# Attention and two expert layers on one core: the build-time estimate that orders the work gets new rules, and the order changes

## The chip, the cores and the metric

The kernel runs on one core of a Trainium2 chip, as one launch. The metric is device time in microseconds (us) of that core. Engines are named as the profile names them: PE (TensorE matmul), PEld (its weight loads), DVE (VectorE), ACT (ScalarE), POOL (GpSimd), SP (SyncE, which issues most transfers).

## The reference

Linear attention with random features, then two mixture-of-experts layers, each of which takes the output of the one before. There are 4 batches, 8 heads, 576 tokens, head size 64, 128 features; the expert layers see 4 x 576 tokens of width 512 and have 8 experts with a hidden width of 1024.

```
def phi(x):                                   # x: (b, h, s, 64)
    h = x @ omega.T - sum(x * x, -1) / 2      # 128 features
    return exp(h - max(h, -1)) / sqrt(128)
kv  = einsum('bhsm,bhsd->bhmd', phi(k), v);   z = phi(k).sum(2)
num = einsum('bhsm,bhmd->bhsd', phi(q), kv);  den = phi(q) . z + 1e-6
x   = num / den
# expert layer 1
e   = argmax(x @ w_gate, 1)
out[mask_e] = prob_e * sigmoid(x @ w_output_gate)[e] * (relu(x[mask_e] @ w1[e]) @ w2[e])
# expert layer 2: the same with its own weights and without the sigmoid
```

## The kernel before

**Tiling.** Attention works on 16 pairs of heads (4 batches of 4 pairs). For a pair it projects the keys (`k_proj`, matmuls `ph<-om,kr`, then a maximum and ten exponentials into `kp`), contracts them with the values (`kv`, `pkv<-vt,kp`), projects the queries (`q_proj`), takes a maximum over partitions on POOL (`qhl<-qhh`), subtracts it on DVE, takes the exponential on ACT (`q_exp`), and contracts with `kv` (`num`, into `pa`); `den_a` to `norm` divide. The table `FORMS` gives each pair one of three forms: F keeps queries and `kv` as whole f32 (`pa<-qhh,kvr`, a matmul that the trace shows as two records); S splits both into a high and a low f32r part (`qh`, `ql`, `kvh`, `kvl`) and takes three products; R keeps it whole with another layout.

**Expert units.** For each layer and batch one unit computes the most frequent expert of the batch densely over its 576 tokens: an up contraction (`pm<-xh,wh`, `pm<-xl,wh`, `pm<-xh,wl`: 512 to 1024, 8 blocks of output, then `hh` on ACT and `hl` on DVE), and a down contraction (`pm<-hh,wh` and its two companions: 8 blocks of `hh` into each of 4 outputs). The 8 units follow each other; the three products in f32r take the place of f32 ones. Weights arrive as `wr`, ACT casts `wh`, DVE subtracts `wl`. The tokens of other experts are gathered in small groups (the `Block` of a layer: `put`, `sel`, the transposes `pst`, down to `pby`) and computed apart.

**What sets the order.** The program is written out once, at build, and each engine runs its list in that order. Between the matmuls of a unit there are slots, and into each slot `Attention.go` (L680) puts the attention step whose key is lowest among those that are admissible. The key is an entry of `WEIGHTS` or `RAW_WEIGHTS`, `PACE[9]` per pair, and a number of `TWEAKS` for that one step. Admissible is a step whose inputs the class `Estimate` (L101) has ready by then; it keeps a clock for each engine, a cost for each instruction, and a time at which each tile is free again. All instructions pass through `Engine.__getattr__` (L197), which is why almost every row of the trace has the line L208. Side streams (the routers `gate`, L729; the Block) advance when the estimate has what they yielded ready. Until the first unit begins, `fill` (L1316) writes an idle matmul on zeros (`idle<-zeros`) wherever nothing is admissible.

**PSUM.** The pool `psa`, tag `pa`, has 7 banks in the start-up and 4 afterwards (L1216, L1363). All of `pa`, `ph`, `pkv`, `pn`, `pg`, `pt`, `pc`, `ptc` and `pst` live there; a key projection takes four of them, two for its first three chunks of 128 tokens and two for the rest, each by half of the features' pair. The expert units have `pm` of their own. In the estimate a new tile takes the place of the one handed out `bufs` tiles before:

```
        if len(names) >= bufs:
            self.before[t.tensor.name] = names[-bufs]
```

**DVE and POOL.** Here the estimate starts a DVE instruction on SBUF no earlier than 1.2 after the start of the latest maximum on POOL (`hold`, L170 and L180).

Of the kernel before, what the change touches and what calls it, by code (L numbers as in the profile page):

```python
# [31 lines left out]
TW = 72  # L32
# [18 lines left out]
ORDER = 3  # L51


FORMS = "FRRRFFFSSSSSSSSS"
CW = 132
XW = 4

WEIGHTS = (-99.0, -99.0, 262.75, -267.46, 198.55, 332.25, -310.29, -471.44, -33.14, 239.82, -489.57, 351.55, -254.05, 173.97)
RAW_WEIGHTS = (-99.0, -99.0, -374.05, -379.93, 519.94, 42.51, 947.74, -153.49, 153.44, 733.35, -182.45, -952.4, -419.2, -198.78)

PACE = (0.097, 0.001, 1.054, 1.126, 886.024, 3.696, 0.265, 0.264, 1.069, 256.941, 0)

COPIES = (1, 1, 2, 1, 0, 0, 2)

START_PACE = (0.142, 0.015, 7.433)
START_COPIES = (1, 2, 0, 1, 0, 0, 0)
TWEAKS = {  # L70
    ("den_a", 1): 44.7, ("den_a", 2): 595.6, ("den_a", 3): -18.8, ("den_a", 4): 323.2, ("den_a", 5): 525.4,
    ("den_a", 6): 291.8, ("den_a", 7): -101.8, ("den_a", 8): -71.9, ("den_a", 9): 56.6, ("den_b", 0): 325.6,
    ("den_b", 1): 1.1, ("den_b", 4): 37.9, ("den_b", 5): -9.0, ("den_b", 6): 171.8, ("den_b", 7): 121.2,
    ("den_b", 8): -64.0, ("den_b", 9): -127.0, ("den_c", 0): 75.6, ("den_c", 1): -98.6, ("den_c", 2): 478.0,
    ("den_c", 4): 37.6, ("den_c", 5): -237.6, ("den_c", 6): -550.8, ("den_c", 9): 0.0, ("den_w", 0): 345.4,
    ("den_w", 1): 143.8, ("den_w", 2): 574.5, ("den_w", 3): -16.2, ("den_w", 4): -57.6, ("den_w", 5): -71.8,
    ("den_w", 6): 77.2, ("den_w", 7): 20.5, ("den_w", 8): 24.7, ("den_w", 9): 7.5, ("k_proj", 0): 107.5,
    ("k_proj", 1): -20.1, ("k_proj", 2): 135.6, ("k_proj", 3): -98.0, ("k_proj", 4): -29.4,
    ("k_proj", 5): -51.0, ("k_proj", 6): -49.7, ("k_proj", 8): 473.1, ("k_proj", 9): -623.2, ("kv", 0): -176.7,
    ("kv", 1): -125.4, ("kv", 3): 483.1, ("kv", 4): -62.8, ("kv", 7): -51.7, ("kv", 8): -203.5,  # L80
    ("kv", 9): 650.0, ("norm", 0): 643.8, ("norm", 1): 542.2, ("norm", 2): 77.4, ("norm", 3): -45.2,
    ("norm", 4): -186.2, ("norm", 5): -106.9, ("norm", 6): 227.5, ("norm", 7): 48.0, ("norm", 8): -0.4,
    ("norm", 9): -5.1, ("num", 0): 0.5, ("num", 1): -19.9, ("num", 10): 26.1, ("num", 14): 416.8,
    ("num", 16): 22.8, ("num", 17): 45.6, ("num", 18): 55.1, ("num", 2): -74.7, ("num", 3): 19.4,
    ("num", 4): -844.8, ("num", 6): 170.0, ("num", 7): -558.5, ("q_cut", 1): -198.8, ("q_cut", 11): -85.3,
    ("q_cut", 12): 60.3, ("q_cut", 13): -72.2, ("q_cut", 14): -1186.5, ("q_cut", 16): -207.1,
    ("q_cut", 17): 478.9, ("q_cut", 19): -174.8, ("q_cut", 2): 25.9, ("q_cut", 3): -306.2, ("q_cut", 4): -287.7,
    ("q_cut", 5): -24.0, ("q_cut", 6): -93.1, ("q_cut", 7): -533.3, ("q_cut", 9): -21.1, ("q_exp", 0): -237.5,
    ("q_exp", 1): 916.5, ("q_exp", 10): -245.4, ("q_exp", 11): -365.4, ("q_exp", 13): -179.8,
    ("q_exp", 14): 179.6, ("q_exp", 15): -1328.8, ("q_exp", 17): 117.8, ("q_exp", 18): 181.2,  # L90
    ("q_exp", 19): -23.4, ("q_exp", 2): 343.6, ("q_exp", 3): -348.5, ("q_exp", 5): -38.0, ("q_exp", 6): -20.7,
    ("q_exp", 7): 4.5, ("q_exp", 9): 820.0, ("q_proj", 0): -488.4, ("q_proj", 1): 984.4, ("q_proj", 10): -817.3,
    ("q_proj", 11): -497.2, ("q_proj", 12): 68.1, ("q_proj", 13): -219.8, ("q_proj", 14): -554.4,
    ("q_proj", 16): -308.5, ("q_proj", 19): 96.0, ("q_proj", 3): -28.6, ("q_proj", 4): -32.0,
    ("q_proj", 5): 11.6, ("q_proj", 6): -43.9, ("q_split", 11): -396.2, ("q_split", 14): -317.9,
    ("q_split", 15): 29.6, ("q_split", 17): -159.4, ("q_split", 18): 101.6, ("q_split", 19): -14.0,
    ("q_split", 5): 27.3, ("q_split", 6): -34.7, ("q_split", 7): -89.0, ("q_split", 9): -848.8,
}


class Estimate:  # L101
# [3 lines left out]
    def __init__(self):  # L105
        self.now = dict.fromkeys(("tensor", "vector", "scalar", "gpsimd", "sync", "dma"), 0.7)
        self.written, self.used, self.slots, self.before = {}, {}, {}, {}
        self.sums = set()

        self.window, self.work, self.slow = 0, 0.0, True  # L110

        self.hold = 0.0

        self.rows = 128

# [2 lines left out]

    def tile(self, ring, bufs, t):

        names = self.slots.setdefault(ring, [])
        if len(names) >= bufs:
            self.before[t.tensor.name] = names[-bufs]
        names.append(t.tensor.name)

    def clock(self, begin):
        while begin >= (self.window + 1) * 3.413:
# [8 lines left out]
    def run(self, engine, op, out, ins):  # L136
# [2 lines left out]
        begin = max(self.now[engine], self.ready(ins), free)  # L139
        psum = any(t.tensor.name in self.sums for t in (out, *ins))  # L140
        if op == "dma_start":
            self.now[engine] = begin + (0.45 if out.shape[0] % 128 == 0 or out.shape[0] < 64 else 0.65)
            end = self.now["dma"] = max(begin + 1.1, self.now["dma"]) + math.prod(out.shape) * 4 / 330e3
            end += 1.0
        elif engine == "tensor":
            if op == "transpose":
# [66 lines left out]
class Pool:  # L213
# [34 lines left out]
def attention_moe_moe_kernel(ctx, tc, qT, qT2, kT, vp, omst, wg1, wg2, w1a, w2a, w1b, w2b, tabs, eye, outT):  # L248
# [354 lines left out]
    class Attention:  # L603
# [15 lines left out]
        def needs(self, kind):  # L619
# [109 lines left out]
    def gate(l, b, x, again=False):  # L729
# [760 lines left out]
```

## Time and profile before

| what | value |
|---|---|
| median of 3 runs | 588.97 us (588.17 to 589.77) |
| profiled execution | 588.86 us |
| its span, first to last instruction | 587.10 us |
| mean granted clock of PE | 0.994 |
| busy: PE, PEld | 567.9 (97%), 540.7 (92%) |
| busy: DVE, ACT, POOL | 371.1 (63%), 225.3 (38%), 68.4 (12%) |
| matmul records of PE | 4519 |
| maxima on POOL | 32, 67.2 us in all |

The page comes first for who is busy; the waits of PE say what ended its idle time; the timeline of PE around such a wait says what stands before and behind it; windows give the granted clock of a stretch.

### The profile page before, as it was taken

Reading aid. Unit: us, or ns where it says so; the run is one execution under the profiler, and the core shown is the slowest. Engines: PE = TensorE matmul, PEld = TensorE weight load, DVE = VectorE, ACT = ScalarE, POOL = GpSimd, SP = SyncE. Lnnn points to the kernel's source line nnn. Section 1 sums busy time; section 2 is a strip of 40 time slices with the busy share of each in tenths; the row PEclk is TensorE's granted clock in tenths of the full one; section 3 lists DMA queues with packets and bytes.
Section 4 is the critical chain, followed back from the end, with each engine's and each line's share of the span. In section 5 each row is a group of like instructions: output and inputs, shape, how many; then the busy total and the mean of one; then the engine's idle time right before and its main releaser. Section 6 shows DMA issues by size and latency. Waiting matters only on the chain.

```text
span 587.1 us, 11426 instructions
## 1 busy us (share of the span) xinstructions
PE 567.9 (97%) x4519; PEld 540.7 (92%) x4519; DVE 371.1 (63%) x695; ACT 225.3 (38%) x503; POOL 68.4 (12%) x48
## 2 busy tenths in 40 slices
PE   8999989999999999999999999999999999999995
PEld 7887779988999999899999999999999999879995
DVE  4487678887775787487866876764545485313522
ACT  6776645224536224424353344322331232324300
POOL 3670500202001130011201210000000000000000
PEclk9999999989999999999999999999999999999998
DMA  9314376525473263283534634544243238664411
GB/s 315 105 62 129 93 231 194 155 87 171 127 171 123 80 217 89 66 272 130 177 94 124 199 103 114 137 150 136 81 118 133 93 95 250 235 218 154 122 41 45
DMA packets 96955, 82.76 MB, mean 141 GB/s; under 512 B 24576, under 2 KB 78464, under 8 KB 96896
## 3 DMA queue, kind: packets, MB, share of 16 engines
q1 hardware_dynamic: 95776, 81.78, 45.1%
q8 instruction: 37, 0.61, 0.4%
q10 hardware_dynamic: 1120, 0.19, 0.2%
q14 instruction: 22, 0.18, 0.1%
HBM read 66.36 MB, written 15.54 MB: 140 GB/s over the span
## 4 chain that ended last, share of the span: by engine, by line
PE 80%; DVE 8%; DMA 5%; issue 3%; ACT 2%; POOL 0%; SPq 0%; ACTq 0%; DVEq 0%; POOLq 0%
PE pm L208 62%; PE pkv L208 5%; PE ph L208 4%; PE pa L208 4%; DMA wr<-w1a 2%; DVE qhh L208 1%; PE pg L208 1%; DMA wr<-w2a 1%; DVE wl L208 1%; DMA qr<-qT 1%; DVE nm L208 1%; ACT wh L208 1%; PE pby L208 1%; DMA rdd<-dt 1%; ACT kp L208 1%
## 5 line engine op out<-in xcount | busy, mean ns | idle before, releaser
L208 PE MATMUL pm<-xh,wh 128*128 128x288 f32 x512 | 113.4, 303 | 1.6 <-DVE hl L208 1.3
L208 PE MATMUL pm<-hh,wh 128*128 128x288 f32 x512 | 114.2, 302 | 0.6 <-DVE y L208 0.6
L208 PE MATMUL pm<-hh,wl 128*128 128x288 f32 x512 | 111.4, 297 | 0.0
L208 PE MATMUL pm<-hl,wh 128*128 128x288 f32 x512 | 111.3, 297 | 0.0
L208 PE MATMUL pm<-xh,wl 128*128 128x288 f32 x512 | 109.6, 296 | 0.5 <-DVE wl L208 0.5
L208 PE MATMUL pm<-xl,wh 128*128 128x288 f32 x512 | 109.5, 295 | 0.0
L208 POOL PARTITION_ALL_REDUCE qhl<-qhh x32 | 67.2, 2139 | 282.8 <-DVE qhh L208 185.2
L208 ACT CAST wh<-wr 128x1024 fp32r<-128x1024 f32 (+1 forms) x72 | 67.8, 951 | 55.5 <-PE pm L208 40.5
L208 PEld LDWEIGHTS pm<-xh,wh 128*128 128x128 f32 x512 | 82.1, 189 | 5.7 <-DVE hl L208 2.3
L208 PEld LDWEIGHTS pm<-hh,wh 128*128 128x128 f32 x512 | 82.9, 190 | 4.4 <-issue 3.0
L208 DVE TENSOR_TENSOR wl<-wr,wh 128x1024 fp32r<-128x1024 f32 (+1 forms) x72 | 78.5, 1103 | 12.6 <-ACT wh L208 12.2
L208 PEld LDWEIGHTS pm<-hh,wl 128*128 128x128 f32 x512 | 83.3, 190 | 0.0
L208 PEld LDWEIGHTS pm<-hl,wh 128*128 128x128 f32 x512 | 83.2, 190 | 0.0
L208 DVE SCALAR_TENSOR_TENSOR hl<-pm,hh 128x576 fp32r<-128x576 f32 x64 | 48.4, 757 | 54.8 <-ACT hh L208 53.9
L208 PEld LDWEIGHTS pm<-xh,wl 128*128 128x128 f32 x512 | 82.4, 188 | 0.7 <-DVE wl L208 0.7
L208 PEld LDWEIGHTS pm<-xl,wh 128*128 128x128 f32 x512 | 82.3, 188 | 0.0
L208 ACT ACTIVATE hh<-pm 128x576 fp32r<-128x576 f32 x64 | 41.7, 651 | 73.3 <-PE pm L208 73.2
L208 DVE TENSOR_TENSOR y<-pm,cb 128x576 f32<-128x576 f32 (+1 forms) x33 | 24.3, 737 | 58.4 <-PE pm L208 58.3
L208 ACT ACTIVATE kp<-ph,nm 128x128 f32<-128x128 f32 x140 | 38.0, 387 | 21.1 <-DVE nm L208 19.2
L208 ACT ACTIVATE qhh<-qhh 128x576 f32<-128x576 f32 x32 | 22.1, 706 | 58.3 <-DVE qhh L208 56.1
L208 DVE TENSOR_REDUCE nm<-ph 128x3 f32<-128x384 f32 (+1 forms) x64 | 27.2, 484 | 14.2 <-PE ph L208 14.1
L208 PEld LDWEIGHTS pkv<-vt,kp 128*128 128x128 f32 x280 | 32.6, 192 | 1.5 <-ACT ev L208 0.8
(145 smaller groups left out, 580.0 us busy)
## 6 DMA issues: line engine op xcount, KB each, us to landing
wr<-w2a SPq DMA_DIRECT2D x16, 512.0 KB, 4.1
wr<-w2b SPq DMA_DIRECT2D x16, 512.0 KB, 3.9
qr<-qT SPq DMA_DIRECT2D x24, 288.0 KB, 4.3
wr<-w1a SPq DMA_DIRECT2D x12, 512.0 KB, 4.7
wr<-w1b SPq DMA_DIRECT2D x12, 512.0 KB, 3.9
vt<-vp SPq DMA_DIRECT2D x16, 325.0 KB, 4.5
kr<-kT SPq DMA_DIRECT2D x16, 288.0 KB, 4.4
xd<-xraw SPq DMA_DIRECT2D x16, 288.0 KB, 3.5
```

Of the source, the lines that this page charges most:

```text
L208: return f(*args, **kw)
```

## The change

The estimate changes in three rules. A new PSUM tile takes, of the banks whose last use is an engine's read, the one read first, instead of a fixed round; a step that needs several banks is admissible only if so many are free (`spare`, `banks`). DVE is held after each of the last eight maxima, not only the last. A transfer's cost goes by the length of its rows. The two exponentials of a router get tiles of their own, `ge` and `te`, where they were slices of `g` and `t`; the router's stream yields those. `FORMS` makes pairs 8 and 10 (batch 2, first and third pair) F instead of S. `WEIGHTS`, `RAW_WEIGHTS`, `PACE`, `COPIES` (which engine copies what), `START_PACE`, `START_COPIES` and `TWEAKS` have other numbers, so that another order results. No transfer and no maximum is added or dropped.

```
-FORMS = "FRRRFFFSSSSSSSSS"
+FORMS = "FRRRFFFSFSFSSSSS"
-COPIES = (1, 1, 2, 1, 0, 0, 2)
+COPIES = (1, 1, 1, 1, 0, 0, 2)
-START_COPIES = (1, 2, 0, 1, 0, 0, 0)
+START_COPIES = (2, 0, 0, 1, 0, 0, 0)
-    ("den_a", 1): 44.7, ("den_a", 2): 595.6, ("den_a", 3): -18.8, ("den_a", 4): 323.2, ("den_a", 5): 525.4,
+    ("den_a", 0): -615.3, ("den_a", 1): -48.5, ("den_a", 2): 148.9, ("den_a", 3): 49.8, ("den_a", 4): -124.6,
...
         names = self.slots.setdefault(ring, [])
         if len(names) >= bufs:
-            self.before[t.tensor.name] = names[-bufs]
+            old = names[0]
+            if self.banks.get(ring):
+                read = [n for n in names if n in self.seen and not self.seen[n][1]]
+                old = min(read, key=lambda n: self.seen[n][0], default=old)
+            names.remove(old)
+            self.before[t.tensor.name] = old
         names.append(t.tensor.name)
+
+    def spare(self, pool, tag):
+
+        ring = id(pool), tag
+        return pool.bufs - sum(n not in self.seen or self.seen[n][1] for n in self.slots.get(ring, ()))
...
-                    self.hold = begin + 1.2
+                    self.holds = [*self.holds[-7:], begin]
...
-                if self.hold - 1.2 < begin < self.hold and not psum:
-                    begin = self.hold
+                for h in self.holds:
+                    if h < begin < h + 1.2 and not psum:
+                        begin = h + 1.2
...
+        self.uses += 1
         for t in (out, *ins):
             name = t.tensor.name
+            self.seen[name] = self.uses, engine == "tensor"
...
+        def banks(self, kind, p):
+            if kind == "k_proj" or kind == "q_proj" and p.tiled:
+                return 4
+            return {"q_proj": 2, "num": 2, "kv": 1, "norm": 2 * p.raw, "q_exp": 2 * p.flip}.get(kind, 0)
...
                 if any(now[e] > now["tensor"] + limit for e in engines):
+                    continue
+                if est.spare(pl.psa, "pa") < self.banks(kind, self.pairs[k]):
                     continue
...
-        nc.scalar.activation(g[:, 2], g[:, 1], AF.Exp)
+        nc.scalar.activation(ge, g[:, 1], AF.Exp)
...
-            nc.scalar.activation(t[:, 5], t[:, 4], AF.Exp, scale=-1.0)
-        yield [g, t]
-        nc.vector.tensor_reduce(out=t[:, 2], in_=g[:, 2], axis=AX.X, op=ALU.add)
+            nc.scalar.activation(te, t[:, 4], AF.Exp, scale=-1.0)
+        yield [ge, te] if l == 0 else [ge]
+        nc.vector.tensor_reduce(out=t[:, 2], in_=ge, axis=AX.X, op=ALU.add)
```

The order on PE around the ninth key projection (pair 8), in the first unit; `pt` is the router's transpose of its logits `lg`, `pm` the unit. Before:

```order
L208 MATMUL pm<-hh,wh 128x288 x2
L208 MATMUL pm<-hl,wh 128x288 x2
L208 MATMUL pm<-hh,wl 128x288 x2
L208 MATMUL pt<-ident,lg 72x128 x2
L208 MATMUL ph<-om,kr 128x128 x10
L208 MATMUL pm<-hh,wh 128x288 x2
```

Now:

```order
L229 MATMUL pa<-qh,kvh 128x288
L229 MATMUL pa<-qh,kvl 128x288
L229 MATMUL pa<-ql,kvh 128x288
L229 MATMUL pm<-xh,wh 128x288 x2
L229 MATMUL pm<-xl,wh 128x288 x2
L229 MATMUL pm<-xh,wl 128x288 x2
L229 MATMUL ph<-om,kr 128x128 x10
L229 MATMUL pm<-xh,wh 128x288 x2
```

The projection has moved from the unit's down contraction into its up contraction, and no router tile stands directly ahead of it. The tenth, which stood behind a `ptc` and a `pkv`, and the thirteenth, which stood behind a `ptc`, now stand behind `pm`; the eleventh stands behind a `pkv` in both.

The order on PE around the first transposes `pst` of the second layer's Block, with tile numbers so that the blocks of `hh` can be counted; the seventh unit's down contraction is under way, and a new pair of `hh`, `hl` begins each block. Before:

```order
L208 MATMUL pm_5994<-hh_5690,wh_5734 128x288 x2
L208 MATMUL pm_5994<-hl_5691,wh_5734 128x288 x2
L208 MATMUL pm_5994<-hh_5690,wl_5735 128x288 x2
L208 MATMUL pm_5994<-hh_5723,wh_5734 128x288 x2
L208 MATMUL pm_5994<-hl_5724,wh_5734 128x288 x2
L208 MATMUL pm_5994<-hh_5723,wl_5735 128x288 x2
L208 MATMUL pst_6032<-ident_89,sel_5944 96x128 x4
L208 MATMUL pm_5994<-hh_5767,wh_5734 128x288 x2
```

Now:

```order
L229 MATMUL pm_5962<-hh_5788,wh_5702 128x288 x2
L229 MATMUL pm_5962<-hl_5789,wh_5702 128x288 x2
L229 MATMUL pm_5962<-hh_5788,wl_5703 128x288 x2
L229 MATMUL pm_5962<-hh_5838,wh_5702 128x288 x2
L229 MATMUL pm_5962<-hl_5839,wh_5702 128x288 x2
L229 MATMUL pm_5962<-hh_5838,wl_5703 128x288 x2
L229 MATMUL pst_6018<-ident_89,sel_5912 96x128 x4
L229 MATMUL pm_5962<-hh_5897,wh_5702 128x288 x2
```

Before, `pst` stood behind the fourth of the output's eight blocks of `hh`; now it stands behind the seventh, so 18 `pm` matmuls later. Between the last `ptc` ahead of it and `pst` there were 162 `pm` matmuls, and there are 180.

The order on DVE at the start of the first unit's up contraction; `xh` and `xl` are the unit's last input parts, `hl` the low part of a hidden block, `dt` a pair's denominators. Before:

```order
L208 TENSOR_TENSOR xl<-xraw,xh 128x576
L208 TENSOR_SCALAR dt<-dt 32x36
L208 RECIPROCAL dt<-dt 32x36
L208 TENSOR_TENSOR qhh<-qhh,qhl 128x576
L208 CAST qh<-qhh 128x576
L208 SCALAR_TENSOR_TENSOR hl<-pm,hh 128x576
L208 TENSOR_TENSOR wl<-wr,wh 128x1024 x2
L208 SCALAR_TENSOR_TENSOR hl<-pm,hh 128x576
```

Now:

```order
L229 TENSOR_TENSOR xl<-xraw,xh 128x576
L229 SCALAR_TENSOR_TENSOR hl<-pm,hh 128x576
L229 TENSOR_SCALAR dt<-dt 32x36
L229 RECIPROCAL dt<-dt 32x36
L229 TENSOR_TENSOR qhh<-qhh,qhl 128x576
L229 CAST qh<-qhh 128x576
L229 TENSOR_TENSOR wl<-wr,wh 128x1024
L229 SCALAR_TENSOR_TENSOR hl<-pm,hh 128x576
```

The first `hl` has moved ahead of a pair's four small and middle instructions; the second still stands behind them, with one `wl` fewer between.

## Rows read from the trace of the kernel before

**Rows 1.** The page's part 1, busy time of each engine.

```profile
PE 567.9 (97%) x4519; PEld 540.7 (92%) x4519; DVE 371.1 (63%) x695; ACT 225.3 (38%) x503; POOL 68.4 (12%) x48
```

**Rows 2.** Windows around 126 us: stretch, length, busy us (instructions), clock, DMA share, GB/s.

```profile
122.80:126.30 3.50, 2.16 (x25) 1.65 (x22) 2.19 (x5) 1.63 (x6) 0.00 (x0) 1.00 0.51 159
126.30:129.70 3.40, 3.40 (x16) 3.40 (x15) 3.26 (x8) 1.31 (x6) 0.00 (x0) 0.50 0.12 18
```

**Rows 3.** Waits of PE: waited for, total us, times, longest.

```profile
PE ph L208 <- ACT kp L208: 4.0, 4, 1.3
PE pm L208 <- DVE hl L208: 1.3, 1, 1.3
PE pst L208 <- issue: 1.2, 1, 1.2
...
PE pn L208 <- ACT qhh L208: 0.5, 1, 0.5
PE pt L208 <- ACT lg L208: 0.4, 1, 0.4
```

**Rows 4.** Timeline of PE, key projections: start, us, instruction, count, idle before.

```profile
123.10 1.16 PE L208 MATMUL ph<-om,kr 64*128 64x128 f32 x14
125.60 0.71 PE L208 MATMUL ph<-om,kr 64*128 64x128 f32 x6 [1.34 <-ACT kp L208]
126.24 0.84 PE L208 MATMUL pm<-hh,wh 128*128 128x288 f32 x2
...
141.19 1.48 PE L208 MATMUL ph<-om,kr 64*128 64x128 f32 x14
143.75 0.71 PE L208 MATMUL ph<-om,kr 64*128 64x128 f32 x6 [1.09 <-ACT kp L208]
144.39 0.53 PE L208 MATMUL pm<-hh,wh 128*128 128x288 f32 x2
...
183.87 1.39 PE L208 MATMUL ph<-om,kr 64*128 64x128 f32 x20
185.18 0.53 PE L208 MATMUL pm<-hh,wh 128*128 128x288 f32 x2
...
233.69 1.16 PE L208 MATMUL ph<-om,kr 64*128 64x128 f32 x14
236.19 0.71 PE L208 MATMUL ph<-om,kr 64*128 64x128 f32 x6 [1.35 <-ACT kp L208]
236.83 0.53 PE L208 MATMUL pm<-xh,wh 128*128 128x288 f32 x2
```

**Rows 5.** Timeline of PE at the state's transposes.

```profile
495.04 0.42 PE L208 MATMUL pm<-hh,wl 128*128 128x288 f32 x2
496.70 0.61 PE L208 MATMUL pst<-ident,sel 128*96 128x128 f32 x4 [1.24 <-issue]
```

**Rows 6.** Timeline of DVE at the same place.

```profile
495.79 0.81 DVE L208 SCALAR_TENSOR_TENSOR sel<-pos,state,sel 128x576 f32<-128x576 f32 x1
```

**Rows 7.** Chain that ended last: start, us, what.

```profile
505.68 1.58 PE pm L208 x12
...
527.53 0.97 PE pby L208 x4
```

**Rows 8.** Timeline of ACT in the start-up.

```profile
18.71 3.92 ACT L208 COPY qhh<-ph 128x288 f32<-128x288 f32 x12 [0.28 <-PE ph L208]
22.40 0.80 ACT L208 ACTIVATE qhh<-qhh 128x576 f32<-128x576 f32 x1
```

**Rows 9.** Timeline of DVE in the first unit.

```profile
82.72 0.76 DVE L208 SCALAR_TENSOR_TENSOR hl<-pm,hh 128x576 fp32r<-128x576 f32 x1
```

**Rows 10.** Tiles qhh and qhl: ns min/median/max, first and last start, form.

```profile
L208 POOL PARTITION_ALL_REDUCE qhl<-qhh x32: 1964/2042/2762, 9.9 to 349.3; - x32
L208 DVE TENSOR_TENSOR qhh<-qhh,qhl x32: 682/751/1706, 11.9 to 353.5; 128x576 f32<-128x576 f32 x32
```

More of the change, by code (lines that the diff above doesn't have):

```diff
@@ L51 @@
 ORDER = 3
-FORMS = "FRRRFFFSSSSSSSSS"
+FORMS = "FRRRFFFSFSFSSSSS"
 CW = 132
 XW = 4
-WEIGHTS = (-99.0, -99.0, 262.75, -267.46, 198.55, 332.25, -310.29, -471.44, -33.14, 239.82, -489.57, 351.55, -254.05, 173.97)
-RAW_WEIGHTS = (-99.0, -99.0, -374.05, -379.93, 519.94, 42.51, 947.74, -153.49, 153.44, 733.35, -182.45, -952.4, -419.2, -198.78)
-PACE = (0.097, 0.001, 1.054, 1.126, 886.024, 3.696, 0.265, 0.264, 1.069, 256.941, 0)
-COPIES = (1, 1, 2, 1, 0, 0, 2)
-START_PACE = (0.142, 0.015, 7.433)
-START_COPIES = (1, 2, 0, 1, 0, 0, 0)
@@ L70 @@
-TWEAKS = {
-    ("den_a", 1): 44.7, ("den_a", 2): 595.6, ("den_a", 3): -18.8, ("den_a", 4): 323.2, ("den_a", 5): 525.4,
[L72 to L97, printed above, removed]
@@ new lines @@
+WEIGHTS = (-99.0, -99.0, 465.22, -215.23, 475.57, 303.97, 62.0, -391.59, -72.09, 241.12, -272.33, 415.93, -220.17, 177.53)
+RAW_WEIGHTS = (-99.0, -99.0, -320.83, -643.41, 757.51, 23.54, 902.27, -181.77, -108.58, 760.71, -209.95, -1003.88, -544.16, -272.35)
+PACE = (0.06, 0.02, 1.043, 1.722, 1746.379, 0.527, 0.544, 0.14, 0.662, 226.645, 0)
+COPIES = (1, 1, 1, 1, 0, 0, 2)
+START_PACE = (0.008, 0.005, 9.732)
+START_COPIES = (2, 0, 0, 1, 0, 0, 0)
+TWEAKS = {
+    ("den_a", 0): -615.3, ("den_a", 1): -48.5, ("den_a", 2): 148.9, ("den_a", 3): 49.8, ("den_a", 4): -124.6,
+    ("den_a", 5): -241.3, ("den_a", 6): 9.0, ("den_a", 7): 58.2, ("den_a", 8): 39.3, ("den_a", 9): 66.5,
+    ("den_b", 0): -22.1, ("den_b", 1): -120.3, ("den_b", 2): -43.5, ("den_b", 3): -30.1, ("den_b", 4): -12.3,
+    ("den_b", 5): -27.2, ("den_b", 6): -186.1, ("den_b", 7): 8.6, ("den_b", 8): -28.8, ("den_b", 9): -156.6,
+    ("den_c", 0): 297.9, ("den_c", 1): 87.7, ("den_c", 2): 7.2, ("den_c", 3): -101.4, ("den_c", 6): 559.4,
+    ("den_c", 7): 122.8, ("den_c", 8): 892.4, ("den_c", 9): -130.8, ("den_w", 0): 65.5, ("den_w", 1): 69.5,
+    ("den_w", 4): -8.8, ("den_w", 7): 55.1, ("den_w", 8): 51.1, ("den_w", 9): 315.7, ("k_proj", 0): 43.7,
+    ("k_proj", 1): 770.1, ("k_proj", 2): 6.2, ("k_proj", 5): -102.0, ("k_proj", 6): -135.9,
+    ("k_proj", 7): -485.8, ("k_proj", 8): 201.5, ("k_proj", 9): -509.3, ("kv", 0): 800.9, ("kv", 2): -971.1,
+    ("kv", 3): 539.0, ("kv", 4): -158.3, ("kv", 5): 14.6, ("kv", 7): -1420.6, ("kv", 8): 133.2, ("kv", 9): 57.6,
+    ("norm", 0): -36.8, ("norm", 1): -2.7, ("norm", 2): -245.3, ("norm", 3): 192.2, ("norm", 5): -251.9,
+    ("norm", 6): -22.2, ("norm", 7): 56.3, ("norm", 9): -21.9, ("num", 0): 259.5, ("num", 1): 239.5,
+    ("num", 12): -74.1, ("num", 13): -3.1, ("num", 14): -402.8, ("num", 15): -45.9, ("num", 17): -1553.0,
+    ("num", 18): 464.6, ("num", 19): -484.1, ("num", 2): 16.8, ("num", 3): -58.4, ("num", 4): -48.5,
+    ("num", 7): -37.5, ("q_cut", 0): 470.8, ("q_cut", 1): 52.5, ("q_cut", 10): 287.1, ("q_cut", 11): 390.2,
+    ("q_cut", 12): -26.4, ("q_cut", 13): 125.3, ("q_cut", 14): 3.7, ("q_cut", 15): 40.2, ("q_cut", 17): 412.5,
+    ("q_cut", 18): 48.1, ("q_cut", 19): -173.6, ("q_cut", 2): -56.2, ("q_cut", 8): -8.2, ("q_exp", 1): 916.5,
+    ("q_exp", 10): 20.8, ("q_exp", 12): -67.8, ("q_exp", 13): -91.1, ("q_exp", 14): 17.5, ("q_exp", 15): -87.5,
+    ("q_exp", 16): -39.0, ("q_exp", 18): 45.7, ("q_exp", 19): 55.4, ("q_exp", 2): 1058.6, ("q_exp", 3): -69.7,
+    ("q_exp", 4): -458.6, ("q_exp", 5): 1030.3, ("q_exp", 7): 82.1, ("q_exp", 8): 1.3, ("q_exp", 9): 291.1,
+    ("q_proj", 1): -49.4, ("q_proj", 10): -249.0, ("q_proj", 11): 20.8, ("q_proj", 12): -127.1,
+    ("q_proj", 13): -109.9, ("q_proj", 14): -554.4, ("q_proj", 15): -192.8, ("q_proj", 16): -104.3,
+    ("q_proj", 2): 1419.6, ("q_proj", 3): -180.4, ("q_proj", 4): 61.9, ("q_proj", 5): -23.2, ("q_proj", 6): 6.8,
+    ("q_proj", 7): 100.9, ("q_proj", 8): -41.2, ("q_proj", 9): -222.4, ("q_split", 0): 27.2,
+    ("q_split", 1): -26.3, ("q_split", 10): -206.2, ("q_split", 11): -4.4, ("q_split", 13): 51.2,
+    ("q_split", 14): -317.9, ("q_split", 15): -589.0, ("q_split", 17): -159.4, ("q_split", 19): 38.5,
+    ("q_split", 2): 20.6, ("q_split", 3): 34.3, ("q_split", 5): -39.3, ("q_split", 6): 615.3,
+    ("q_split", 7): -40.6, ("q_split", 8): -7.0, ("q_split", 9): 848.8,
@@ L108, in __init__ @@
         self.sums = set()
+        self.banks, self.seen, self.uses = {}, {}, 0
         self.window, self.work, self.slow = 0, 0.0, True
-        self.hold = 0.0
+        self.holds = []
         self.rows = 128
@@ L141, in run @@
         if op == "dma_start":
-            self.now[engine] = begin + (0.45 if out.shape[0] % 128 == 0 or out.shape[0] < 64 else 0.65)
-            end = self.now["dma"] = max(begin + 1.1, self.now["dma"]) + math.prod(out.shape) * 4 / 330e3
+            self.now[engine] = begin + (0.42 if out.shape[0] % 128 == 0 else 0.55)
+            row = out.shape[-1] * 4
+            cost = math.prod(out.shape[:-1]) / 16e3 * (2 + row / 25 if row >= 512 else 40 if row > 256 else 10)
+            if len(out.shape) > 2 and row >= 512 or out.shape[0] == 64:
+                cost *= 1.5
+            end = self.now["dma"] = max(begin + 1.1, self.now["dma"]) + max(0.17, cost)
             end += 1.0
@@ L219, in tile @@
         t = self.pool.tile(shape, dtype, tag=tag, name=name, **kw)
+        self.estimate.banks[id(self), tag] = self.space is not None
         self.estimate.tile((id(self), tag), bufs or self.bufs, t)
@@ L754, in gate @@
         ls = pl.mp.tile([TW, NT, GW], F32, tag="ls", name="ls", bufs=1)
+        ge = pl.mp.tile([TW, NT, E], F32, tag="ge", name="ge", bufs=1)
+        te = pl.mp.tile([TW, NT, 1], F32, tag="te", name="te", bufs=1)
         first = rev[:TW]
@@ L812, in gate @@
             nc.vector.scalar_tensor_tensor(
-                out=t[:, 3], in0=t[:, 5], scalar=1.0, in1=t[:, 3], op0=ALU.add, op1=ALU.mult
+                out=t[:, 3], in0=te, scalar=1.0, in1=t[:, 3], op0=ALU.add, op1=ALU.mult
             )
```

## The prediction

> **What bounds the kernel now.** I read the page's busy times first. PE is busy 567.9 us of a span of 587.10 [rows 1], so 19.2 us at most can be won without taking work off PE; DVE, at 63%, and the others bound nothing on average. So I listed what ended PE's waits [rows 3]. The largest entry is the key projection `ph`, which waits for the exponentials `kp` four times, 4.0 us in all. The other single waits of a size that matters are one for `hl` in the first unit (1.3) and one before `pst` (1.2); what else the view lists are waits of half a microsecond, such as `pn` (0.5) and `pt` (0.4).
>
> Next, the timeline of PE at those projections [rows 4]. A projection is 20 records. One that meets no wait starts at 183.87 and the next `pm` at 185.18: 1.31 us. The ninth stops after 14 records, waits 1.34 us for `kp`, and the next `pm` starts at 126.24, that is 3.14 us after 123.10. A projection fills four banks, two of three chunks each and two of two chunks; its seven first matmuls need three of them, the eighth the fourth. That is where the records break, 14 and 6: the fourth bank was still held by what stood directly ahead (a router's `pt`, not yet read), so the eighth matmul had to take the projection's own first bank, once its exponentials were done. The same picture stands at 141.19 (3.20) and 233.69 (3.14), where a `pkv` and a `ptc` stood ahead.
>
> Last, the granted clock. Between the start-up and the end it dips once, and the windows place that: 3.50 us at 1.00 with PE busy 2.16, then 3.40 us at 0.50, that is 1.2 GHz instead of 2.4, with PE busy throughout [rows 2]. The first of these stretches holds the ninth projection's stall.
>
> **The change part by part.** The sum is made against the profiled execution, 588.86 us (the span 587.10 and 1.76 around it); the median of the runs is 0.11 above, and I carry the sum over to the median.
>
> *Key projections.* By the new order the ninth, tenth and thirteenth no longer stand behind a router's tile or a `pkv`; a `pm` block lies ahead, during which older banks are read out. What they cost over a free one is 3.14 - 1.31 = 1.83, 3.20 - 1.31 = 1.89, and 1.83 again [rows 4]: 5.55 us, all on PE's path, since PE has nothing else in its list there. The eleventh stands behind a `pkv` before and after, so I count no change for it. What is late next at the ninth is the next `hh` cast or DVE's `hl`, neither of which the timeline shows waiting when the projection runs through. Value -5.55, bounds -5.55 and -4.5 (a short wait of 0.35 left at each of three).
>
> *The half clock.* 3.40 us at half the clock do the work of 1.70 [rows 2]. If the stall ahead of it goes, so does this: -1.7, bounds -1.7 and 0. By the rows, three stalls of 1.09 to 1.35 us at key projections brought one such stretch, so the coincidence is one in three here. Beside that stands a rule of the Trainium skill, "TensorE: Matmul & The Clock Gate", Part 1: The HAM clock gate: throttled is the default and activity releases it, and the monitor's window runs freely, so where a stall falls decides as much as how long it is. The trace agrees as far as one in three goes; the rule speaks against the full 1.7, since a new stall elsewhere may fall badly, and by it the gain would be 1.7 smaller. That result is the first rival below.
>
> *The `pst` wait.* Before, `pm` x2 starts at 495.04 and at 0.132 a matmul (12 in 1.58 [rows 7]) would end at 495.30; `pst` starts at 496.70, 1.40 later [rows 5], because `sel` on DVE ends at 495.79 + 0.81 = 496.60 [rows 6]. Now `pst` stands 18 `pm` later, 18 x 0.132 = 2.37 us, and the order ahead of `sel` on DVE and of its transfer is as before. So 2.37 - 1.40 = 0.97 us to spare, and the wait goes: -1.40. Nothing in the Block behind `pst` had less slack than that: the next groups of it are not in the waits [rows 3]. Bounds -1.4 and -0.8, if `sel` comes 0.6 later still beyond the slack.
>
> *Two pairs in form F.* Pairs 8 and 10 lose 24 f32r products, 24 x 0.132 = 3.17 us, and gain 8 f32 ones of two records. A record of f32 with the same 288 columns takes 0.97 / 4 = 0.24 (`pby` [rows 7]): 16 x 0.2425 = 3.88. So +0.7 on PE; the nearest lower value, if a record of `pa` overlaps its neighbour, gives 0. DVE loses four casts, four subtractions and two of `kvl`, but it bounds nothing there: no gain counted. I take +0.7, bounds 0 and +0.7.
>
> *Start-up.* The count of idle matmuls falls from 54 to 42, but these fill waits and cost nothing by themselves. On ACT, the exponential `qhh` at 22.40 stood behind 12 copies of `ph` [rows 8]; now only 8 of these come before it, 4 x 3.92 / 12 = 1.31 us less of copies, while an exponential moves ahead of them, 0.80. So -0.5 (bounds -1.3, if that exponential finds ACT idle, and +0.5, if the filler that went leaves PE to wait where it did not). The rest of the start-up ends on the chain of routers and first weights, in which nothing changed. What hides the change of order there is that chain; if it is earlier by 1.3, that is the lower bound.
>
> *First unit.* The first `hl` ends its wait earlier: it started at 82.72 behind `dt`, `qhh` and `qh` [rows 9] and made PE wait 1.3 [rows 3]. It now stands ahead of them. The second `hl` stands behind them instead, with one `wl` less between. DVE has the same list of work up to there but for that `wl`, so the wait may only be handed on by a block. 0, bounds -1.3 and +1.3.
>
> *The router's tiles, the estimate's other rules.* `ge` and `te` change when the estimate holds the exponentials for ready; on the chip the same two instructions write the same amount. 0. The new costs of transfers and the holds work through the order only, which is priced above.
>
> *New small waits.* The small waits of before belong to its order; a new order has its own. Rows of that size are 0.4 and 0.5 [rows 3]. I add three of 0.45, +1.3, bounds 0 and +2.5, and give no credit for the old ones.
>
> Sum: -5.55 - 1.7 - 1.4 + 0.7 - 0.5 + 0 + 1.3 = -7.15. So 588.97 - 7.15 = 581.8 us. With all lower ends (-5.55 - 1.7 - 1.4 + 0 - 1.3 - 1.3 + 0 = -11.25) it would be 577.7; with a middle run of upper ends (-4.5, -0.8, +0.7, +0.5, 0, +2.5 and the clock at -1.7: -3.3) 585.7. Both ends together are unlikely; the forecast's own range is 579 to 585.7.
>
> **The rivals.**
>
> *The half clock moves instead of vanishing.* For it: a single stall of some 1.3 us in one of three places was enough. The fewer idle matmuls in the start-up leave PE to wait on exponentials, where such a stretch may begin. Against it: 54 fillers before included ones that changed nothing in the clock. Time: 581.8 + 1.7 = 583.5. Chance 0.2.
>
> *The order does not free the banks.* The bank rule is one of the estimate; on the chip the pool and the readers decide. If the eighth matmul still waits at three projections, the 5.55 and the 1.7 stay: -1.4 + 0.7 - 0.5 + 1.3 = +0.1, so 589.1. For it: the change at L116 touches no instruction. Against it: the order itself has moved those three. Chance 0.08.
>
> *DVE falls behind in the first unit (slower).* Mechanism: the first unit now carries key projections nine to eleven, the ninth in its up contraction, so DVE has their maxima, subtractions and casts to do while each block of the up contraction needs an `hl` from it. A subtraction `qhh` that meets a maximum on POOL has taken up to 1.706 us against a median of 0.751, 0.96 more [rows 10]. Each `hl` that comes late costs PE what the one late `hl` did, 1.3 [rows 3]. With all 8 blocks late, 8 x 1.3 = 10.4: -7.15 + 10.4 = +3.25, so 592.2. It decides from the sixth late block on (7.15 / 1.3 = 5.5). For it: the ninth projection's work on DVE moves from the down contraction into the up one, where `hl` and `wl` are due. Against it: two pairs less to split, and one late `hl` in eight before. Chance 0.1. Beside this, the Trainium skill, "SBUF — State Buffer", Who interferes with whom, says that a DVE instruction with two inputs in SBUF contends with a GpSimd instruction that reads SBUF, over one shared port pair, and that the loser blocks until the other ends. The longest `qhh` agrees with a block of part of a maximum; by the rule it could wait a whole maximum, 2.04 in the median [rows 10], and then four late blocks would do, 4 x 2.04 = 8.2 against 7.15.
>
> **How the numbers follow.** Forecast 0.6, clock moved 0.2, banks not freed 0.08, DVE late 0.1, better than the forecast's range 0.02. What can be told from no change is 0.3%, 1.8 us: faster is below 587.2, slower above 590.7. Faster: 0.6 + 0.2 + 0.02 = 0.82; of that 0.01 I move to the same, for a forecast whose upper ends all fall together: 0.81. Same: 0.08 + 0.01 = 0.09. Slower: 0.1. The range of 8 in 10 leaves out the slower case and most of the unfreed banks: 578.5 to 587.5.
>
> **What would show it.** Right: no wait of `ph` for `kp` over 0.5 us behind the first unit's start; 20 records of each later projection within 1.3 to 1.7 us; full clock from the start-up to the end; no wait ahead of `pst`; PE's busy time, idle matmuls aside, about 1.0 us lower, with 1.7 off for the clock and 0.7 on for form F. Wrong: waits of `pm` for `hl` or `wl` that sum to more than 3 us, a stretch at 0.50, or `ph` rows that come in 14 and 6 again.

## The result and the profile after

The changed kernel takes 582.43 us, the median of 4 runs (580.02 to 584.09), against 588.57 for the kernel before beside it: a ratio of 0.9891, 95% interval 0.9856 to 0.9926. The forecast was 581.8 with 578.5 to 587.5. The profiled execution took 584.09 us (span 582.3), the slowest of the four, so the rows below come to 4.8 us less than the span before, not to the median's 6.1.

The page's busy time of PE hardly changes, 567.4 us against 567.9, so most of the 4.8 us are waits:

```profile
PE 567.4 (97%) x4499; PEld 539.9 (93%) x4499; DVE 365.4 (63%) x685; ACT 222.6 (38%) x503; POOL 67.7 (12%) x48
```

In the waits of PE (waited for, total us, times, longest) `kp` falls from 4.0 to 0.6, and that 0.6 is in the start-up; `pst` is gone. Against [rows 3] `hl` has grown; `y` stood at 0.6 before, and `kr` (a key load, by DMA) is new:

```profile
PE pm L229 <- DVE hl L229: 2.2, 3, 1.3
PE pm L229 <- DVE y L229: 1.5, 2, 1.0
...
PE ph L229 <- DMA kr<-kT: 0.8, 1, 0.8
PE ph L229 <- ACT kp L229: 0.6, 1, 0.6
```

Of the kernel before, these small waits are gone from the list as well, besides `pn` and `pt`:

```profile
PE pa L208 <- ACT xraw L208: 0.6, 1, 0.6
...
PE pa L208 <- ACT wh L208: 0.5, 1, 0.5
...
PE pa L208 <- ACT kp L208: 0.4, 1, 0.4
PE pa L208 <- DVE ql L208: 0.3, 1, 0.3
PE pa L208 <- DVE qhh L208: 0.2, 1, 0.2
```

The timeline of PE at the ninth, tenth and eleventh key projection answers to [rows 4]:

```profile
97.74 0.94 PE L229 MATMUL ph<-om,kr 64*128 64x128 f32 x12
98.87 1.01 PE L229 MATMUL ph<-om,kr 64*128 64x128 f32 x8 [0.19 <-ACT ev L229]
99.81 0.53 PE L229 MATMUL pm<-xh,wh 128*128 128x288 f32 x2
...
114.77 0.42 PE L229 MATMUL pm<-hh,wl 128*128 128x288 f32 x2
116.01 1.39 PE L229 MATMUL ph<-om,kr 64*128 64x128 f32 x20 [0.81 <-DMA kr<-kT]
117.32 0.53 PE L229 MATMUL pm<-hh,wh 128*128 128x288 f32 x2
...
123.73 1.70 PE L229 MATMUL ph<-om,kr 64*128 64x128 f32 x20
125.36 0.53 PE L229 MATMUL pm<-hh,wh 128*128 128x288 f32 x2
```

None of the sixteen stops after 14 records any more. The ninth needs 99.81 - 97.74 = 2.07, 0.76 over a free one, with a short wait for `ev` (a bank whose reader is late). The tenth runs through, but starts at 116.01 where the `pm` ahead of it, at 114.77, would have let it start at 115.03: its keys came 0.81 us late by the view. The eleventh, behind its `pkv`, is as it was. The timeline of SP shows the load of those keys:

```profile
108.15 2.75 SPq L229 DMA_DIRECT2D qr<-qT  x2
110.95 1.20 SPq L229 DMA_DIRECT2D kr<-kT  x1
```

At `pst` the PE does not stop, and `sel` on DVE ends at 492.79 + 0.81 = 493.60, half a microsecond ahead [rows 5, 6]:

```profile
493.83 0.42 PE L229 MATMUL pm<-hh,wl 128*128 128x288 f32 x2
494.10 0.60 PE L229 MATMUL pst<-ident,sel 128*96 128x128 f32 x4
```

On DVE, `sel` of the changed kernel:

```profile
492.79 0.81 DVE L229 SCALAR_TENSOR_TENSOR sel<-pos,state,sel 128x576 f32<-128x576 f32 x1
```

The granted clock did not stay up. The windows (as in [rows 2]) show the half clock, 1.2 GHz, for two stretches of the start-up, right behind one in which PE was busy 2.77 of 3.40:

```profile
35.50:38.90 3.40, 2.77 (x17) 1.83 (x16) 3.30 (x5) 3.40 (x15) 1.89 (x1) 1.00 0.01 3
38.90:42.30 3.40, 3.40 (x18) 3.40 (x18) 3.19 (x8) 1.23 (x3) 0.59 (x1) 0.51 0.76 242
42.30:45.70 3.40, 3.40 (x18) 3.34 (x16) 3.13 (x5) 0.90 (x3) 3.32 (x2) 0.50 0.07 22
```

### The profile page after: what moved, and what is told of

The parts are those of the page before. It is cut to its first block, busy times and chain, and to the rows that moved or that the text cites. A ratio compares the mean times of both kernels' runs of the same rounds, so it can differ in the third digit from the quotient of the medians.

```text
span 582.3 us, 11386 instructions
## 1 busy us (share of the span) xinstructions
PE 567.4 (97%) x4499; PEld 539.9 (93%) x4499; DVE 365.4 (63%) x685; ACT 222.6 (38%) x503; POOL 67.7 (12%) x48
## 4 chain that ended last, share of the span: by engine, by line
PE 80%; DVE 9%; DMA 4%; ACT 3%; issue 2%; SPq 0%; ACTq 0%
PE pm L229 60%; PE pkv L229 5%; PE ph L229 5%; PE pa L229 4%; DVE wl L229 2%; DVE qhh L229 1%; DVE hl L229 1%; PE pg L229 1%; PE pn L229 1%; ACT wh L229 1%; DMA wr<-w1a 1%; ACT qhh L229 1%; DMA wr<-w2a 1%; DMA kr<-kT 1%; DVE xraw L229 1%
## 5 line engine op out<-in xcount | busy, mean ns | idle before, releaser
L229 PEld LDWEIGHTS pkv<-vt,kp 128*128 128x128 f32 x280 | 34.8, 202 | 1.5 <-ACT ev L229 0.8
```

The costliest lines, as they stand in the source:

```text
L229: return f(*args, **kw)
```

## The experiments

To change one thing at a time, the order that each kernel's estimate chose was written out as a list of decisions, which the kernel then follows. The experiments edit single entries of that list. (Where the estimate itself is changed, in the rules and the numbers, there is no such list.) "9th" to "14th" below are key projections.

**Three key projections moved (in the kernel before).**

```
 MATMUL pt<-ident,lg x2
-MATMUL ph<-om,kr x10            9th, now 30 pm later, behind pc
 ... MATMUL pkv<-vt,kp x10
-MATMUL ph<-om,kr x10            10th, now 12 pm later
 ... MATMUL ptc<-ident,g
-MATMUL ph<-om,kr x10            13th, now 12 pm later
```

> The kernel before, its order written out as it was, with one edit: the ninth, tenth and thirteenth key projection stand 6 to 18 pm matmuls later, so that the router's tile or pkv ahead of them has been read. Bank theory: each projection runs through (20 records in one piece), 1.83 + 1.89 + 1.83 = 5.55 us go, and the half clock behind the ninth too (1.7) unless another stall brings it back; 588.6 - 5.55 = 583.0, at best 581.3. Rival (the wait belongs to ACT's exponentials being late in that part of the kernel, wherever the projection stands): waits of ph for kp stay at 1.1 to 1.3, no change, 588.6.

Measured: 588.0 us, ratio 0.9986 (0.9966 to 1.0005): next to nothing. (The ninth was moved by 30 `pm`, not by 6 to 18.) The timeline of PE gives a part of the reason:

```profile
127.40 1.39 PE L249 MATMUL ph<-om,kr 64*128 64x128 f32 x20
...
132.61 0.58 PE L249 MATMUL pa<-qs,omsth 128*128 128x288 f32 x1 [2.02 <-ACT kp L249]
```

The ninth runs through now, but 12 `pm` later stands a query projection, `pa<-qs,omsth`, which needs a bank and waits 2.02 us for the same exponentials. A projection holds all four banks until its exponentials are done, so whatever needs a bank behind it waits too. Of the forecast's mechanism one half was missing: the tile ahead is not all that counts. But 2.0 us handed on would leave 3.5 of the 5.55, and the tenth and the thirteenth run through. The windows show another part:

```profile
134.00:136.00 2.00, 1.97 (x8) 1.62 (x8) 0.79 (x2) 1.86 (x6) 1.08 (x1) 0.50 0.36 134
136.00:138.00 2.00, 2.00 (x10) 2.00 (x9) 1.86 (x5) 0.22 (x1) 2.00 (x2) 0.50 0.00 0
```

Behind the wait the clock is at half from about 132.6 to 139.4, twice as long as in the kernel before. The mean clock is at 0.995 or less in 9 of these 12 runs, against 16 of the 33 of the kernel before beside them. How much of the missing gain the clock took is not measured.

**The `pst` moved (in the kernel before).**

```
+MATMUL pm x18                   three blocks of hh, from behind phf
 MATMUL pst<-ident,sel x4
```

> The kernel before with the Block's first pst 18 pm matmuls later and nothing else earlier or later than three slots. Theory: the 1.40 us wait ahead of pst goes and nothing behind it becomes late: 588.6 - 1.4 = 587.2, within what timing can tell from no change, so the trace decides: no wait at pst. Rival (the Block's chain from pst to pby is on the path to the end): the steps behind it come 2.4 us later and the end with them, 588.6 to 589.6, with a new wait at pxg, pu or pby.

Measured: 586.7 us, ratio 0.9963 (0.9938 to 0.9988): the wait is gone, and its 1.4 us lie within the interval. The trace shows one thing more. The ninth projection stalls as before, and the clock behind it stays at 1.00. The timeline of PE:

```profile
123.08 1.16 PE L249 MATMUL ph<-om,kr 64*128 64x128 f32 x14
125.58 0.71 PE L249 MATMUL ph<-om,kr 64*128 64x128 f32 x6 [1.34 <-ACT kp L249]
```

And the windows of that execution:

```profile
122.80:126.20 3.40, 2.06 (x23) 1.56 (x21) 1.86 (x5) 1.56 (x6) 0.00 (x0) 1.00 0.44 136
126.20:129.60 3.40, 3.40 (x27) 3.39 (x27) 3.27 (x8) 1.38 (x6) 0.00 (x0) 1.00 0.06 19
```

The same stall is followed by a half-clock stretch in one execution and by none in another.

**The two forms (in the kernel before).**

```
-FORMS = "FRRRFFFSSSSSSSSS"
+FORMS = "FRRRFFFSFSFSSSSS"
```

> The kernel before, its order written out, with pairs 8 and 10 whole in f32 and nothing else. Theory: PE's work grows by 16 x 0.2425 - 24 x 0.132 = 0.7 us, DVE loses about 7 us of work that hid beside PE: 588.6 + 0.7 = 589.3 (same by timing). Rival (DVE's relief ends waits in the units): 586 to 587.

Measured: 588.88 us, ratio 0.9997 (0.9977 to 1.0016). The two pairs in F neither pay nor cost what timing can tell; 0.7 is inside the interval. In its trace eight records of `pa<-qhh,kvr` in a row take 2.10 us, 0.26 each, near the 0.24 of the forecast. The rival, 586 to 587, did not come about.

**The two moves together (in the kernel before).**

```
 the edits of the first and the second experiment
```

> The kernel before with the two edits together, the three key projections and the pst. Theory: 588.6 - 5.55 - 1.4 = 581.7, at best 580.0 where no half clock falls, which is the time of the changed kernel (582.4): then four moved steps out of hundreds are the whole gain. Rival (the rest of the new order carries part of the gain): 584 to 586.

Measured: 586.19 us, ratio 0.9956 (0.9934 to 0.9979), of which the `pst` is most. As in the first experiment, the ninth projection's wait was still there, under another name (`pa` for `kp`, 2.0 us), and a half-clock stretch stood behind it.

**The four moves, with the ninth put where banks are free (in the kernel before).**

```
-MATMUL ph<-om,kr x10            9th, now 66 pm and a pg earlier
 ... 10th, 13th and pst as above
```

> The kernel before with four steps moved: the ninth key projection to 84 pm matmuls earlier, where no step that needs a bank follows for 7 us, the tenth and thirteenth 6 to 12 pm later as in the last trial, and pst 18 pm later. In the last trial the ninth stood ahead of a query projection, which then waited 2.0 us for the same exponentials. Bank theory with that corrected (a projection holds all four banks until its exponentials are done, so what counts is what needs a bank on either side of it): none of the three waits nor a wait of pa for kp over 0.5 us remains, 588.9 - 5.5 - 1.4 = 582.0, 580.5 to 583.5. Rival (the waits are handed on again, to the next bank user or to hl): 585 to 587.

Measured: 583.52 us, ratio 0.9915 (0.9895 to 0.9934). The timeline of PE shows the three projections:

```profile
112.34 1.39 PE L249 MATMUL ph<-om,kr 64*128 64x128 f32 x20
...
141.02 1.16 PE L249 MATMUL ph<-om,kr 64*128 64x128 f32 x14
142.69 0.71 PE L249 MATMUL ph<-om,kr 64*128 64x128 f32 x6 [0.52 <-ACT ct L249]
143.33 0.53 PE L249 MATMUL pm<-xh,wh 128*128 128x288 f32 x2
...
233.06 1.39 PE L249 MATMUL ph<-om,kr 64*128 64x128 f32 x20
```

The ninth and the thirteenth run through; the tenth still waits 0.52 us for a `ct` that is read late and takes 2.31, 1.0 over a free one. So 5.55 - 1.0 + 1.4 = 5.95 was to be had. The median is 589.42 - 583.52 = 5.9 lower, but the ratio makes it 5.0 (3.9 to 6.2), and none of these six runs has a mean clock of 0.995 or less, against 13 of the 22 of the kernel before beside them; against those of the 22 at 0.997 or more, with a median of 588.75, it is 5.2. Four steps moved in the old order give most of the gain of the whole change: 0.85% against 1.09%, with intervals that overlap.

**More idle matmuls in the start-up (in the changed kernel).**

```
 MATMUL ph<-om,kr x10
+MATMUL idle<-zeros x6
 MATMUL ph<-qr,om x4
```

> The changed kernel with six more idle matmuls in the start-up, ahead of the query projection whose last matmul waits 0.61 us for kp (there the profiled execution of the changed kernel fell to half the clock, from 39.0 to 45.7 us, 3.4 us lost). They take time in which PE waited. Theory (the stall brings the half clock): the stretch between 36 and 46 us keeps 1.00, median 0 to 2 us under the changed kernel's 582.4. Rival (the low clock there doesn't hang on that stall): the clock falls in some execution as before, and the fillers cost 0 to 0.7 us: 582.4 to 583.

Measured: 581.65 us, ratio 0.9873 (0.9841 to 0.9906), against 0.9891 without them: not told apart by time. In the profiled execution the clock stays up (windows):

```profile
39.40:42.80 3.40, 3.40 (x32) 3.40 (x32) 3.19 (x8) 1.22 (x3) 0.56 (x1) 1.00 0.73 248
42.80:46.20 3.40, 3.21 (x36) 2.83 (x34) 3.13 (x5) 0.90 (x3) 3.35 (x2) 1.00 0.61 192
```

but two of the six runs show a mean clock of 0.993 against 0.996 to 0.998 in the others, so low stretches still come in some executions. That the fillers keep them off is not shown: the next experiment, without them, has the same 2.77 of 3.40 busy ahead of that place as the changed kernel, and its profiled execution keeps its clock there too.

**Three steps moved in the changed kernel.**

```
-MATMUL ph<-om,kr x10                    10th, 6 pm later
-TENSOR_TENSOR qhh<-qhh,qhl  (DVE)       behind the second hl
-TENSOR_REDUCE gt<-ge and six more (DVE) behind y, xh, xl
```

> The changed kernel with three steps moved: the tenth key projection 6 pm later (its keys arrived 0.81 us late), a query exponential of the first unit behind the second hl (1.29 us wait of pm), a router's last step behind the unit's y (0.96 us wait). Theory (new waits of the new order, each removable by itself): 0.8 + 1.3 + 1.0 = up to 3.1 us less, 579.3. Rival (each wait is handed on to the next hl, y or transfer): 582.4, with waits of 1 us at the neighbours.

Measured: 583.72 us, ratio 0.9907 (0.9874 to 0.994): no gain that timing can tell. The wait for the keys is gone, the two others were handed on (timeline of PE):

```profile
88.52 0.53 PE L270 MATMUL pm<-xh,wh 128*128 128x288 f32 x2 [1.46 <-DVE hl L270]
...
153.07 0.25 PE L270 MATMUL ptc<-ident,g 72*64 72x72 f32 x1 [1.36 <-DVE g L270]
```

The `hl` wait of 1.29 at 87.18 has become one of 1.46 a block later, and the wait for `y` one of `ptc` for `g`, which the moved router step writes.

**Two projections put back behind unread tiles (in the changed kernel).**

```
 MATMUL pt<-ident,lg x2
+MATMUL ph<-om,kr x10            11th, from behind pkv
 ... MATMUL ptc<-ident,g
+MATMUL ph<-om,kr x10            14th, 12 matmuls earlier
```

> The changed kernel with the eleventh and the fourteenth key projection moved to stand directly behind a router's tile (pt, ptc) that has not been read. Bank theory: both stop after 14 records and wait 1.1 to 1.35 us for their own kp, 1.8 us each less the 0.3 they lost before: 582.4 + 3.3 = 585.7, more if the half clock falls. Rival (in the new order ACT is less loaded, so that exponentials come in time): no wait over 0.5, 582.4.

Measured: 590.55 us, ratio 1.003 (1.0002 to 1.0058): two steps out of the whole order lose more than the change gained, 590.55 - 582.43 = 8.1 us, more than twice the 3.3 expected. The timeline of PE:

```profile
132.30 0.94 PE L270 MATMUL ph<-om,kr 64*128 64x128 f32 x12
135.18 0.49 PE L270 MATMUL ph<-om,kr 64*128 64x128 f32 x2 [1.94 <-DVE qhh L270]
136.62 0.71 PE L270 MATMUL ph<-om,kr 64*128 64x128 f32 x6 [0.95 <-ACT kp L270]
...
244.61 1.16 PE L270 MATMUL ph<-om,kr 64*128 64x128 f32 x14
248.16 0.71 PE L270 MATMUL ph<-om,kr 64*128 64x128 f32 x6 [2.40 <-ACT kp L270]
```

Both stop, the fourteenth after 14 records for 2.40 us, the eleventh twice (1.94 for the subtraction of another tile, then 0.95 for `kp`). Together 5.3 us of waits; in the runs the mean clock went as low as 0.983, against 0.991 to 0.998 in the changed kernel, so low stretches probably have a part in the rest.

**The routers' exponentials as slices again (in the changed kernel).**

```
-ge = tile(...); te = tile(...)
+ge, te = g[:, 2], t[:, 5]
```

> The changed kernel with the routers' exponentials as slices of g and t again, in the same order. Theory: nothing on the chip hangs on it, span and waits as in the changed kernel within 1 us (578 to 584 by its own spread). Rival (the tiles of their own end a false wait): a new wait of g or gt of 0.5 us or more on PE.

Measured: one run, 582.99 us, span 581.2, no wait for `g` or `gt` in PE's list. That is the time of the changed kernel within its own spread, so nothing is seen to hang on these tiles on the chip; one run can't say more.

**The rules alone, and the numbers alone.**

```
 rules alone:    new Estimate, banks(), ge/te;  old FORMS, WEIGHTS ... TWEAKS
 numbers alone:  old Estimate, no banks();      new FORMS, WEIGHTS ... TWEAKS
```

> The changed kernel's estimate (banks by release, holds, transfers) and router tiles with all numbers and FORMS of the kernel before: the rules alone. The order then has no key projection that waits for its own exponentials. Theory (the bank rule alone takes the 5.5 us away, the numbers find the rest): 583 to 586. Rival (an order from numbers that were not made for these rules loses elsewhere what it gains): 588 or more, with waits of other kinds, at hl, wl or transfers.

Measured: 591.04 us, ratio 1.0039 (1.0013 to 1.0064). By its waits of PE no projection stops for `kp` over 0.2 us, as the rule wants it, but one stops after 14 records for 1.8 us for another tile's reader (`kvl`), and time is lost elsewhere:

```profile
PE pm L228 <- ACT wh L228: 4.3, 1, 4.3
...
PE ph L228 <- DVE kvl L228: 1.8, 1, 1.8
...
PE ph L228 <- ACT kp L228: 0.5, 2, 0.2
```

The largest is a single 4.3 us for `wh`, ACT's cast of weights, which stands behind ten `kp` exponentials there. The half clock is in it too. The windows show it around that wait:

```profile
152.00:158.00 6.00, 2.76 (x12) 2.69 (x13) 3.68 (x7) 4.66 (x13) 0.00 (x0) 0.50 0.06 6
```

and all nine runs have a mean clock of 0.992 or less, which only some of the kernel before have. So how much of the loss is the order's waits and how much the clock that came with them stays open.

> The estimate and router tiles of the kernel before with all numbers and FORMS of the changed one: the numbers alone. The order then has three key projections (tenth, eleventh, sixteenth) that take their own first bank. Theory: about 1.8 us for each, 582.4 + 5.5 = 588 or more. Rival (the numbers carry the gain without the rules): 582 to 584.

Measured: 586.63 us, ratio 0.9954 (0.9933 to 0.9975). With the old rules three projections (tenth, eleventh, sixteenth) stop after 14 records again, for their own first bank, and the `pst` wait is there as well (waits of PE):

```profile
PE ph L209 <- ACT kp L209: 4.3, 4, 1.4
PE pst L209 <- issue: 1.4, 1, 1.4
```

So neither half carries the change: the rule finds orders in which projections don't stop for their own exponentials, and the numbers, which were found under that rule, give one of them in which little else stops.

**Five steps moved in the changed kernel.**

```
+MATMUL idle<-zeros x6                   start-up, as above
-MATMUL ph<-om,kr x10                    9th and 10th, 6 pm later; 9th's kv with it
-TENSOR_REDUCE gt<-ge and six more (DVE) behind y, xh, xl
-MATMUL ptc<-ident,g                     18 pm later
```

> The changed kernel with six idle matmuls in the start-up, the ninth key projection (0.95 us over a free one) 6 pm later and its kv with it, the tenth 6 pm later (its keys came 0.81 late), a router's last step behind the unit's y (0.96 wait) and its ptc 18 pm later, so that this wait isn't handed on. Theory: 0.75 + 0.8 + 1.0 less and less half clock in the start-up, 579.5 to 580.5. Rival (handed on to hl or ptc as in the last trial): 581.7 to 583.

Measured: 579.4 us (577.75 to 581.37), ratio 0.9849 (0.9827 to 0.9871), against 0.9891 (0.9856 to 0.9926) for the changed kernel: the fastest of all, clear of the kernel before, but the two intervals overlap, so the gain over the changed kernel is likely and not shown. The waits of PE show what went: `y` is down to 0.6, the keys' and `ev`'s waits are not listed, and the `ptc` that had taken over the wait in the trial above has time enough:

```profile
PE pm L270 <- DVE hl L270: 1.5, 3, 0.5
...
PE pm L270 <- DVE y L270: 0.6, 1, 0.6
```

## Why the prediction was right, and where it was not

The forecast of 581.8 lies 0.6 under the measured median, but its terms did not all come as written.

*Key projections, -5.55 on paper.* The rival by which the banks would not come free fell: no projection behind the start-up waits for its own `kp`. The mechanism is shown from both sides: three stops that go when the projections are moved to where banks are free (-5.0 by the ratio, -5.9 by the medians, with `pst`), stops that return when two are put back. The size was off: the bounds were -5.55 and -4.5, and the rows after show 0.76 left at the ninth and 0.98 at the tenth, so 5.55 - 1.74 = 3.8. The tenth's was no bank but its keys: its load stood in SP's queue behind two query loads (108.15, 2.75 us), of which the second was issued only when DVE's `qs` had ended, and the projection had moved ahead. Moved back by 6 `pm`, it no longer waits for them. The prediction counted the transfers of a moved step at nothing. It was also silent on what stands behind a moved projection; in the changed kernel nothing there is seen to lose by it, in the first experiment it lost 2.0 us.

*The half clock, -1.7.* This step failed. "If the stall ahead of it goes, so does this" took one execution's low stretch for a property of that stall. The same stall brought none in two other traces, those of the `pst` and of the two forms, and the changed kernel's profiled execution had 6.8 us of it in the start-up. The prediction itself lists a stretch at 0.50 among what would show it wrong. Nor was it a single accident: the profiled executions with two projections put back and with the routers' slices are at 0.50 in the same 38.90 to 42.30, and of the four that share this start-up order only the one with three steps moved is not. That is the first rival's case. By the Trainium skill's rule on the clock gate ("TensorE: Matmul & The Clock Gate", Part 1: The HAM clock gate) the window runs freely, so that runs of one kernel differ; the measurement agrees, with mean clocks of 0.991 to 0.998 in the four runs of the changed kernel. What the stretch cost can be read at the first unit's third group of `pm`. In the timeline of PE of the changed kernel:

```profile
74.31 0.53 PE L229 MATMUL pm<-xh,wl 128*128 128x288 f32 x2 [0.35 <-DVE wl L229]
```

In that of the kernel with three steps moved, whose start-up has the same order and kept its clock:

```profile
72.48 0.53 PE L270 MATMUL pm<-xh,wl 128*128 128x288 f32 x2 [0.35 <-DVE wl L270]
```

And in the kernel before:

```profile
73.17 0.53 PE L208 MATMUL pm<-xh,wl 128*128 128x288 f32 x2 [0.50 <-DVE wl L208]
```

74.31 - 72.48 = 1.8 us, not the 3.4 that two stretches of 3.4 at half the clock would give; that the rest fell into time in which PE waited anyway is likely, and not shown. The number is rough: the two other low executions have this group at 74.18 and 74.49, and two with fillers, one start-up order and a full clock have it at 73.02 and 71.59. What a low clock goes with in the median can be read in the kernel before: of its 72 runs beside the experiments, 35 with a mean clock of 0.997 or more have a median of 588.3, and 34 with 0.995 or less one of 590.1. So 1.7 was near the size for one execution, but the stretch comes in about half of them, and the changed kernel has its own.

*`pst`, -1.4.* Right: the wait is gone, with 0.97 to spare on paper and 0.50 in the trace, and the single move gives 0.9963 (0.9938 to 0.9988).

*Form F, +0.7.* Not contradicted; 0.9997 with an interval that holds +0.12%, and the records take the time that was forecast.

*Start-up, -0.5.* By the same rows, 72.48 with a full clock against 73.17 before: -0.7, but one execution each, where executions of one start-up differ by up to 1.4.

*First unit, 0.* Right in its reason. The wait for the first `hl` was handed on: in the changed kernel it stands at 87.18, 1.29 us, and when the subtraction `qhh` ahead of it was moved too, at 88.52. The rival that DVE falls behind in every block did not come about: waits for `hl` sum to 2.2 us.

*New small waits, +1.3.* This term failed in sign. New are 0.9 more for `hl`, 0.9 more for `y` and 0.4 more for `kp` in the start-up, 2.2 in all (`kr` and `ev` are counted with the projections); gone are `pn` 0.5 and `pt` 0.4 [rows 3], 2.0 of `pa`, and 0.2 of `wl` (0.5 to 0.3), 3.1 in all. So -0.9 where the forecast had +1.3: it counted new waits and gave no credit for the old ones. These 2.2 cover the 1.7 that the projections fell short of and part of the 1.7 of the clock, so that the median came out 0.6 from the forecast is partly luck.

The sum of the waits listed (without those of the first microseconds, for `zeros` and `om`) falls from 10.5 to 5.6 us. That is about the 4.8 of the span; what the low clock, the F pairs and the start-up add beside it is not separated.

*Open:* what makes a stall bring a low stretch in one execution and not in the next, whether fillers help against it, and how much of the gain of each moved step is its wait and how much the clock behind it.

## What to carry to other kernels

A step that fills every bank of a pool stalls by what stands on either side of it: an unread tile ahead makes it wait for its own readers, and the next bank user behind inherits the wait. Count banks free at both ends before moving it, and the place of its loads in their queue too. A rule in a scheduler and the numbers found under that rule are one change; tried alone, the rule cost 0.4% here, and the numbers gave 0.5% where both gave 1.1%.

## What the runs showed of the hardware

The mean granted clock of executions of one and the same program differs: 0.992 to 0.999 over the 72 runs of the kernel before beside the experiments, with 586.5 to 592.8 us. Which program it is changes the share of executions with a mean clock of 0.995 or less: 34 of those 72, but 9 of 10 with two projections put back and 9 of 9 with the rules alone. The smaller groups point the same way, and could be chance: 9 of 12 and 7 of 10 where the ninth projection's wait stood ahead of a query projection, 2 of 10 in the kernel that differs from the one before by the `pst` alone, and none of 6 with all four moves. So a low stretch in one profile is a sample: its cost in the median is a share of it, and that share can't be read from one trace.
